# VectorE's order of work at the change to the second MLP, and the place of one ScalarE copy

## The chip, the cores and the metric

The kernel runs on one core of a Trainium2 chip. The metric is the device time of one execution in microseconds. Before the change it is 630.34 us, the median of three runs (629.96 to 630.46).

## The reference

Windowed attention with a position bias, then two layers of feed-forward work on the same 1152 tokens of 512 features. Cut to what matters:

```python
x = attention(q, k, v)                      # 1152 x 512
p = domain_probs / (domain_probs.sum(-1, keepdims=True) + 1e-09)
out = 0                                     # first MLP: 4 experts, 512 -> 1024 -> 512
for e in range(4):
    out += p[:, e:e+1] * (np.maximum(x @ w1[e], 0.0) @ w2[e])
h = out @ w_in                              # second MLP: 512 -> 2048 -> 512
g = h * np.cos(h)
return g @ w_out
```

## The kernel before, in words

Both MLPs run over groups `g` of 512 hidden features: groups 0 to 7 are the four experts (`NG1` = 8), groups 8 to 11 the second MLP. Each float32 operand is held as two parts, a rounded first part (`hi`) and the rest (`lo`); a product is three matmuls of parts (`PASSES`, L730). ScalarE makes first parts with a copy; VectorE or GpSimd makes second parts with a subtraction (`sub`, L190).

The tokens are nine tiles of 128. Tile 0 goes alone (`left`, x0). The other eight make two columns `c` = 1, 2 of 512 tokens, and the product with `w1` or `w_in` is made by seven products of 2 x 2 blocks in place of eight (`pair`). Its right-hand operands are B11, B21, B22 and the differences T1 to T4; each has two slices `m` = 0, 1 of 128 features. They lie in `xs` (B11, T2, T1, T3, B21) and `xz` (B22, T4).

**The stage of the change** is group 7 (`turn` in `steps`). There the output of the last expert is made feature by feature: `features(g, c, d)` runs 12 matmuls into one PSUM bank, for column `c` and feature block `d`; its bank is called D*cd* here, so D20 is column 2, block 0. After the matmuls VectorE multiplies by the expert's share (L1042) and adds the sum of the former experts (L1043). What follows depends on the bank, with `m = d % 2`:
- column 1 (`own`): first part of B11 (d < 2) or B21 (d >= 2), a copy of the bank to SBUF (`keep`, L1052), later the second part;
- column 2, d < 2 (`upper`): `keep`, t1 = column 2 minus column 1, T1's first and second part;
- column 2, d >= 2 (`lower`): t2, t3 on VectorE, first and second parts of T2, B22, T3, then t4 = kept value minus t2, and T4's parts.

The order is written out by hand, `(0, "D10", "f", "D20", "D12", "D22", "D11", "D21", "D13", "D23")`; "f" transposes tile 0 and makes x0. `last_flip` follows with the first products of group 8: `early[0]` (first product of pair 0), `early[1]` (of pair 1), the first half of `left`, then the second product of pair 0, the second half of `left`, the second product of pair 1. The second product adds onto the first one's bank, so it waits for ScalarE's copy `p1` of that bank (L838 in `pair`; the trace calls the tile `p`). Second products read B21; later ones T2, T1, T3, B22, T4 in that order.

Every engine runs its own instructions in the order in which the program issues them. `run` drives the steps: the step's matmuls, then `move(2)`, then `advance()` (the chains of the cosine), weight jobs, and the rest of the step. `features` issues the first piece of its generator at once and puts the generator into `moved`; `move(2)` issues up to two more pieces at the start of the next step:

```python
next(step)
move(2)
for _ in range(stages):
    advance()
for _ in range(njobs):
    next(jobs)
...
next(step, None)
```

Instructions of different engines on one PSUM bank run one after the other, in the order of issue.

Of the kernel before, what the change touches and what calls it, by code (L numbers as in the profile page):

```python
# [52 lines left out]
def tile_kernel(ctx, tc, qT, kT, v, probs, w_1, w_2, w_in, w_out, out):  # L53
    nc = tc.nc
# [134 lines left out]
    def sub(eng, out, a, b):  # L189
        eng.tensor_tensor(out=out, in0=a, in1=b, op=ALU.subtract)  # L190
# [157 lines left out]
    B11, T2, T1, T3, B21, B22, T4 = range(7)  # L348
# [62 lines left out]
    def stage(which=None):  # L411

        for st in list(staged) if which is None else [staged[which]]:
            if next(st, True):
                staged.remove(st)

    moved = []

    def move(n):

        while moved and n:
            if next(moved[0], True):
                moved.pop(0)
            else:
                n -= 1

    def split(out, src, eng):

# [275 lines left out]
    def flush():  # L704

        for out, src, hi in second_parts:
            nc.vector.scalar_tensor_tensor(  # L707
                out=out, in0=src, scalar=0.0, in1=hi.bitcast(F32), op0=ALU.max, op1=ALU.subtract
            )
        second_parts.clear()  # L710
# [38 lines left out]
    def sums():  # L749
        return bank([128, 512], "o_ps")  # L750
# [162 lines left out]
    def ahead(g, t):  # L913

        opened[g, t] = sums()
        tile_matmuls(opened[g, t], g, t, range(NFG // 2))
        yield
# [88 lines left out]
    def x_of(c, d):  # L1006

        x = accpair[:, (c - 1) * NP : c * NP].rearrange("p b (t d e) -> p (b t) d e", t=4, e=32)
        return x[:, :, d]
# [12 lines left out]
            share_rows.append(r)  # L1022

    differences = {}

    def features(g, c, d):

        flush()
        ps = sums()
        for f in range(NFG):  # L1030
            for a, bb in PASSES:
                nc.tensor.matmul(
                    ps, w_t[2, g, f // 2][:, a, f % 2, d * 128 : (d + 1) * 128],
                    hpair[:, bb, f, (c - 1) * NB : c * NB],
                    start=(f == 0 and (a, bb) == PASSES[0]),
                    stop=(f == NFG - 1 and (a, bb) == PASSES[-1]),
                )
        yield
        m, low = d % 2, d >= 2
        squares = lambda t: t.rearrange("p (t e) -> p t e", e=32)  # L1040
        x, kept = squares(ps), x_of(c, d)
        nc.vector.tensor_tensor(out=ps, in0=ps, in1=share_rows[c - 1], op=ALU.mult)  # L1042
        nc.vector.tensor_tensor(out=x, in0=x, in1=kept, op=ALU.add)  # L1043

        def hi(k, src):
            nc.scalar.activation(out=squares(operand_of_x(0, k)[:, m]), in_=src, func=AF.Copy)  # L1046

        def lo(k, src, eng):
            sub(eng, squares(operand_of_x(1, k)[:, m]), src, squares(operand_of_x(0, k)[:, m]).bitcast(F32))

        def keep():
            nc.scalar.activation(out=kept, in_=x, func=AF.Copy)  # L1052

        def difference(name):
            return squares(csp.tile([128, NB], F32, name=name, tag="c"))

        def own(k):
            hi(k, x)
            keep()
            yield  # L1060
            lo(k, x, nc.vector)

        def upper():
            keep()
            t1 = differences[m] = difference("t1")
            sub(nc.vector, t1, x, x_of(1, d))
            hi(T1, t1)
            yield
            lo(T1, t1, nc.gpsimd)

        def lower():
            t2, t3, t4 = difference("t2"), x_of(2, m), x_of(1, d)
            sub(nc.vector, t2, x, differences[m])
            sub(nc.vector, t3, x, t3)
            hi(T2, t2)
            hi(B22, x)
            yield
            lo(T2, t2, nc.gpsimd)
            lo(B22, x, nc.vector)
            hi(T3, t3)  # L1080
            yield
            lo(T3, t3, nc.gpsimd)
            sub(nc.vector, t4, t4, t2)
            hi(T4, t4)
            yield
            lo(T4, t4, nc.vector)

        ch = own(B21 if low else B11) if c == 1 else lower() if low else upper()
        next(ch)
        moved.append(ch)  # L1090

    mm = None
    count = [0]
# [23 lines left out]
    def steps(g):  # L1117

        last, turn = g == NG1 + NG2 - 1, g == NG1 - 1
        moe = g < NG1
        early_kind = 1 if g in (0, NG1) else 0 if moe else 2
        ps = [early.pop(j, None) or pair(g, j, early_kind) for j in range(2)]
        if g == 0:
            yield ahead(0, 0), 0, 0, 0
            for p in ps:
                next(p)
            seq = [0, 1, 0, 1, 0, 0, 1, 0, "0", 1, 1]
            more = [1, 1, 0, 0, 0, 0, 0, 2, 1, 0, 0]  # L1130
        elif g == NG1:
            seq = [0, 0, 0, 0, "X", 0, 1, 1, 1, "0", 1, 1]
            more = [0, 1, 1, 0, 0, 0, 0, 0, 0, 0, 0, 0]
        elif moe:
            seq = [0] * 4 + ["X"] + [0] * 3 + [1] * 7
            more = [0, 1, 1, 0, 0, 0, 0, 0] + [0, 1, 1, 1, 1, 1, 1]
        else:
            seq = [0] * 7 + ["0"] + [1] * 7
            more = [0, 1, 1, 0, 0, 0, 0, 0] + ([0] * 7 if last else [0, 1, 1, 0, 0, 0, 0])
        for j, m in zip(seq, more):  # L1140
            if j == "X":
                yield turn_rows(g), 0 if shuffled(g) else 2, m, 0
            elif j == "0":
                yield layer2(g, 0), 2, m, 0
            else:
                yield ps[j], 1, m, 0
        nxt = None if last else left(g + 1)
        ncv = {0: 2, 5: 3, 6: 3, 1: 3, "La": 3, 7: 3, 2: 3, 8: 3}
        if turn:
            order = (0, "D10", "f", "D20", "D12", "D22", "D11", "D21", "D13", "D23")  # L1150
            njobs = [2, 2, 0, 2, 2]
        elif moe:
            order = (0, 5, 6, 1, "La", "Lb", 7, 2, 8, 3, 4)
            njobs = [1] * 8
            if g == 0:
                order = (5, 6, 1, "La", "Lb", 7, 2, 8, 3, 4)
                njobs[:3] = [2, 2, 2]
                ncv = {5: 1, 6: 2, 1: 3, "La": 1, 7: 3, 2: 3, 8: 3}
        elif last:
            order, njobs = ("a5", "a6", "a7", "a8", "a1", 5, 6, 7, 8, 1, 2, 3, 4), []  # L1160
        else:
            order = ("a5", "a6", "a7", "a8", "a1", "a2", 5, 6, 7, "La", 8, "Lb", 1, 2, 3, "X", 4)
            njobs = [0, 0, 0, 0, 0, 0, 1, 1, 1, 1, 1, 1, 1, 1, 1, 1, 2]
            if g == NG1:
                njobs[4:6] = [1, 1]
        for k, o in enumerate(order):
            m = njobs.pop(0) if njobs else 0
            if nxt and shuffled(g + 1):
                if o == 2:
                    store_rows(g + 1)  # L1170
                if order[k - 1] == 2:
                    load_rows(g + 1)
            if isinstance(o, int):
                assert o == 0 or not any(c > 0 for c, _ in chains)
                yield layer2(g, o), 2, m, ncv.get(o, 0)
            elif o[0] == "f":
                yield flip(), 0, m, 0
            elif o[0] == "D":
                yield features(g, int(o[1]), int(o[2])), 2, m, 0
            elif o[0] == "a":  # L1180
                yield ahead(g, int(o[1])), 2 if last else 1, m, 0
            elif o[0] == "L":
                yield half(nxt, o == "Lb"), 2, m, ncv.get(o, 0)
            else:
                yield turn_rows(g + 1), 2, m, 0
        if turn:
            yield from last_flip(g + 1, nxt)

    def last_flip(g, nxt):

        early.update({j: pair(g, j, 1) for j in range(2)})
        yield early[0], 0, 0, 0
        yield early[1], 0, 0, 0
        yield half(nxt, False), 0, 0, 0
        yield early[0], 1, 0, 0
        yield half(nxt, True), 0, 0, 0
        yield early[1], 2, 0, 0

    def run(groups):
        for g in groups:  # L1200
            for step, stages, njobs, ncv in steps(g):
                next(step)
                move(2)
                for _ in range(stages):
                    advance()
                for _ in range(njobs):
                    next(jobs)
                for _ in range(ncv):
                    next(cv, None)
                next(step, None)  # L1210
                if g in (NG1 - 2, NG1 - 1):
                    fetch_acc(2 if g == NG1 - 2 else 0)
    with tc.manual_schedule():
# [11 lines left out]
        early = {}  # L1225
# [3 lines left out]
        def opening(j, kind):  # L1229
            early[j] = pair(0, j, kind)  # L1230
            return early[j]
# [93 lines left out]
        rest = sum(1 for _ in cv)  # L1325
# [61 lines left out]
```

## Time and profile before

| | us |
|---|---|
| median of three runs | 630.34 |
| the profiled execution | 628.96 |
| its span | 627.2 |
| TensorE busy | 615.1 |
| VectorE busy | 455.6 |
| GpSimd busy | 349.8 |
| ScalarE busy | 322.0 |

The span goes from the first to the last instruction in the profile. In the rows PE is TensorE's matmuls, PEld its weight loads, DVE VectorE, ACT ScalarE, POOL GpSimd. A timeline row gives the start, the time taken, the engine, line, operation, output<-inputs, shape and count; behind it in brackets stands how long the engine was idle before, and who ended that. Several instructions alike stand in one row.

### The profile page before, as it was taken

Reading aid. Unit: us, or ns where it says so; the run is one execution under the profiler, and the core shown is the slowest. Engines: PE = TensorE matmul, PEld = TensorE weight load, DVE = VectorE, ACT = ScalarE, POOL = GpSimd, SP = SyncE. Lnnn points to the kernel's source line nnn. Section 1 sums busy time; section 2 is a strip of 40 time slices with the busy share of each in tenths; the row PEclk is TensorE's granted clock in tenths of the full one; section 3 lists DMA queues with packets and bytes.
Section 4 is the critical chain, followed back from the end, with each engine's and each line's share of the span. In section 5 each row is a group of like instructions: output and inputs, shape, how many; then the busy total and the mean of one; then the engine's idle time right before and its main releaser. Section 6 shows DMA issues by size and latency. Waiting matters only on the chain.

```text
span 627.2 us, 9374 instructions
## 1 busy us (share of the span) xinstructions
PE 615.1 (98%) x3348; PEld 504.1 (80%) x3348; DVE 455.6 (73%) x783; ACT 322.0 (51%) x674; POOL 349.8 (56%) x332
## 2 busy tenths in 40 slices
PE   8999999999999999999999999996999999999998
PEld 6777888888888888888888888884878888888886
DVE  6878898689799799698698645667574664664663
ACT  6989444434434444434442521544783683673660
POOL 4868495463573464464554561673359479379340
PEclk9999999999999999999999999998999999999999
DMA  9641236256348158157163237420101202202003
GB/s 269 176 157 40 93 120 190 56 155 221 94 153 268 49 173 264 38 179 205 36 215 120 66 102 222 147 68 1 34 1 35 100 0 68 67 1 68 15 4 134
DMA packets 51246, 69.05 MB, mean 110 GB/s; under 512 B 6912, under 2 KB 31488, under 8 KB 51200
## 3 DMA queue, kind: packets, MB, share of 16 engines
q1 hardware_dynamic: 50656, 68.06, 35.0%
q8 instruction: 26, 0.43, 0.3%
q10 hardware_dynamic: 544, 0.39, 0.2%
q14 instruction: 20, 0.16, 0.1%
HBM read 53.76 MB, written 14.68 MB: 109 GB/s over the span
## 4 chain that ended last, share of the span: by engine, by line
PE 90%; DVE 4%; ACT 4%; POOL 1%; issue 1%; ACTq 0%; DVEq 0%; POOLq 0%
PE o_ps L923 43%; PE o_ps L730 35%; PE o_ps L784 5%; PE x_ps L571 2%; PE t_ps L535 1%; PE s_ps L465 1%; DVE o_ps L1043 1%; DVE o_ps L1042 1%; PE r_ps L509 1%; PE o_ps L1219 1%; ACT p L484 1%; ACT xs L1046 1%; ACT accpair L1052 1%; DVE xs L190 0%; PE o_ps L963 0%
## 5 line engine op out<-in xcount | busy, mean ns | idle before, releaser
L923 PE MATMUL o_ps<-w2t,hpair 128*128 128x512 f32 x1044 | 241.4, 389 | 0.0
L923 PEld LDWEIGHTS o_ps<-w2t,hpair 128*128 128x128 f32 x1044 | 195.7, 188 | 40.6
L730 PE MATMUL o_ps<-xs,w1t 128*128 128x512 f32 x720 | 170.2, 392 | 6.0 <-ACT p L838 6.0
L730 PEld LDWEIGHTS o_ps<-xs,w1t 128*128 128x128 f32 x720 | 135.5, 189 | 35.2 <-ACT p L838 6.4
L190 POOL TENSOR_TENSOR w2t<-raw,w2t 128x512 fp32r<-128x512 f32 x48 | 63.5, 1338 | 78.5 <-ACT w2t L214 78.4
L190 POOL TENSOR_TENSOR w1t<-raw,w1t 128x512 fp32r<-128x512 f32 x48 | 64.5, 1362 | 62.0 <-ACT w1t L214 61.6
L190 POOL TENSOR_TENSOR w1t<-sm,w1t 128x512 fp32r<-128x512 f32 x48 | 63.8, 1346 | 31.3 <-ACT w1t L214 31.0
L730 PE MATMUL o_ps<-xz,w1t 128*128 128x512 f32 x288 | 69.8, 390 | 0.1
L190 POOL TENSOR_TENSOR hpair<-u,hpair 128x512 fp32r<-128x512 f32 x30 | 40.2, 1348 | 52.4 <-ACT hpair L688 52.4
L313 ACT ACTIVATE cr<-cr 128x512 f32<-128x512 f32 x32 | 21.7, 679 | 81.7 <-DVE ca L307 81.7
L730 PEld LDWEIGHTS o_ps<-xz,w1t 128*128 128x128 f32 x288 | 53.8, 188 | 11.8 <-DVE c L832 0.7
L707 DVE SCALAR_TENSOR_TENSOR hpair<-o_ps,hpair 128x512 fp32r<-128x512 f32 x47 | 32.3, 688 | 19.2 <-ACT hpair L716 19.1
L716 ACT ACTIVATE hpair<-o_ps 128x512 fp32r<-128x512 f32 x47 | 28.0, 595 | 33.6 <-DVE o_ps L832 33.5
L214 ACT ACTIVATE w1t<-sm 128x512 fp32r<-128x512 f32 x44 | 27.6, 629 | 32.6 <-POOL sm L190 32.6
L944 DVE SCALAR_TENSOR_TENSOR accpair<-o_ps,pr,accpair 128x512 f32<-128x512 f32 x48 | 34.8, 745 | 10.4 <-PE o_ps L923 10.4
L672 DVE SCALAR_TENSOR_TENSOR u<-r,u 128x512 f32<-128x512 f32 x36 | 28.1, 781 | 15.9 <-ACT r L669 15.9
L784 PE MATMUL o_ps<-w1t,x 128*128 128x512 f32 x144 | 36.0, 393 | 0.0
L952 DVE TENSOR_TENSOR accpair<-o_ps,accpair 128x512 f32<-128x512 f32 x23 | 15.7, 689 | 27.8 <-PE o_ps L923 27.8
L832 DVE TENSOR_TENSOR o_ps<-o_ps,u 128x512 f32<-128x512 f32 x48 | 33.1, 692 | 3.0 <-PE o_ps L730 2.8
L923 PE MATMUL o_ps<-w2t,h 128*128 128x512 f32 x144 | 34.7, 389 | 0.0
L316 DVE SCALAR_TENSOR_TENSOR co<-cr,ca 128x512 f32<-128x512 f32 x32 | 33.4, 1043 | 1.4 <-ACT cr L313 0.4
L484 ACT ACTIVATE p<-p,nmax 128x192 f32<-128x192 f32 (+1 forms) x72 | 31.0, 436 | 4.7 <-DVE nmax L478 4.6
(147 smaller groups left out, 892.8 us busy)
## 6 DMA issues: line engine op xcount, KB each, us to landing
raw<-w SPq DMA_DIRECT2D x32, 512.0 KB, 4.4
cr<-w_in SPq DMA_DIRECT2D x16, 512.0 KB, 4.5
cr<-w_out SPq DMA_DIRECT2D x16, 512.0 KB, 4.2
wi<-co SPq DMA_DIRECT2D x16, 256.0 KB, 3.4
wo<-co SPq DMA_DIRECT2D x16, 256.0 KB, 2.2
raw<-wi SPq DMA_DIRECT2D x8, 512.0 KB, 3.5
raw<-wo SPq DMA_DIRECT2D x8, 512.0 KB, 3.7
qt<-qT SPq DMA_DIRECT2D x8, 256.0 KB, 4.2
```

Source lines behind the costliest of these rows:

```text
L190: eng.tensor_tensor(out=out, in0=a, in1=b, op=ALU.subtract)
L214: nc.scalar.activation(out=out, in_=src, func=AF.Copy)
L316: nc.vector.scalar_tensor_tensor(out=fl(o), in0=fl(hw), scalar=TINY, in1=fl(a), op0=ALU.is_ge, op1=ALU.mult,)
L484: nc.scalar.activation(out=p[:, k], in_=p[:, k], func=AF.Exp, scale=-1.0, bias=nmax[:, k : k + 1], accum_out=den[:, k, 0:1],)
L672: nc.vector.scalar_tensor_tensor(out=u, in0=r, scalar=MAGIC, in1=u, op0=ALU.subtract, op1=ALU.subtract)
L707: nc.vector.scalar_tensor_tensor(out=out, in0=src, scalar=0.0, in1=hi.bitcast(F32), op0=ALU.max, op1=ALU.subtract)
L716: nc.scalar.activation(out=hi, in_=src, func=AF.Relu)
L730: nc.tensor.matmul(ps, w(a, k, m), operand_of_x(bb, b)[:, m], start=(start and m == 0 and (a, bb) == PASSES[0]), stop=(stop and m == 1 and ...
L784: nc.tensor.matmul(ps.rearrange("p (j f) -> p j f", j=2), x0[:, bb, d, :], w1[:, :, a, 0, d * 256 : (d + 1) * 256], start=(d == 0 and (a, ...
L832: add = lambda out, a, b: nc.vector.tensor_tensor(out=out, in0=a, in1=b, op=ALU.add)
L923: nc.tensor.matmul(ps, hidden(a, f, t), w_t[2, g, f // 2][:, bb, f % 2, :], start=(f == 0 and (a, bb) == PASSES[0]), stop=(f == NFG - 1 an ...
L944: nc.vector.scalar_tensor_tensor(out=o, in0=ps, scalar=s, in1=o, op0=ALU.mult, op1=ALU.add)
```

## The change

`moved` and `move` go, so no pieces are issued ahead of a bank's own work. A bank's sums and differences are issued first; second parts are put into a list, `seconds`, and `second_of_before()` issues the former bank's at a fixed place behind the sums. In `upper`'s case `keep` now comes after the difference. B21's second part of slice 1 is made by GpSimd, from the kept copy; T4's second parts are made by GpSimd too. The last bank, D23, stops after its differences (`yield`), and `opening` in `last_flip` issues the copy of pair 0's first product first, then the rest of D23.

```diff
--- before.py
+++ after.py
@@ -413,16 +413,6 @@
         for st in list(staged) if which is None else [staged[which]]:
             if next(st, True):
                 staged.remove(st)
-
-    moved = []
-
-    def move(n):
-
-        while moved and n:
-            if next(moved[0], True):
-                moved.pop(0)
-            else:
-                n -= 1
 
     def split(out, src, eng):
 
@@ -1022,6 +1012,11 @@
             share_rows.append(r)
 
     differences = {}
+    seconds = []
+
+    def second_of_before():
+        while seconds:
+            seconds.pop(0)()
 
     def features(g, c, d):
 
@@ -1054,40 +1049,42 @@
         def difference(name):
             return squares(csp.tile([128, NB], F32, name=name, tag="c"))
 
-        def own(k):
+        if c == 1:
+            second_of_before()
+            k = B21 if low else B11
             hi(k, x)
             keep()
-            yield
-            lo(k, x, nc.vector)
-
-        def upper():
-            keep()
+            if low and m:
+                lo(k, kept, nc.gpsimd)
+            else:
+                seconds.append(lambda: lo(k, x, nc.vector))
+        elif not low:
             t1 = differences[m] = difference("t1")
             sub(nc.vector, t1, x, x_of(1, d))
+            second_of_before()
             hi(T1, t1)
-            yield
+            keep()
             lo(T1, t1, nc.gpsimd)
-
-        def lower():
+        else:
             t2, t3, t4 = difference("t2"), x_of(2, m), x_of(1, d)
             sub(nc.vector, t2, x, differences[m])
             sub(nc.vector, t3, x, t3)
+            second_of_before()
+            if m:
+                yield
             hi(T2, t2)
             hi(B22, x)
-            yield
+            hi(T3, t3)
             lo(T2, t2, nc.gpsimd)
-            lo(B22, x, nc.vector)
-            hi(T3, t3)
-            yield
             lo(T3, t3, nc.gpsimd)
-            sub(nc.vector, t4, t4, t2)
-            hi(T4, t4)
-            yield
-            lo(T4, t4, nc.vector)
-
-        ch = own(B21 if low else B11) if c == 1 else lower() if low else upper()
-        next(ch)
-        moved.append(ch)
+
+            def rest():
+                lo(B22, x, nc.vector)
+                sub(nc.vector, t4, t4, t2)
+                hi(T4, t4)
+                lo(T4, t4, nc.gpsimd)
+
+            seconds.append(rest)
 
     mm = None
     count = [0]
@@ -1176,7 +1173,8 @@
             elif o[0] == "f":
                 yield flip(), 0, m, 0
             elif o[0] == "D":
-                yield features(g, int(o[1]), int(o[2])), 2, m, 0
+                last_features = features(g, int(o[1]), int(o[2]))
+                yield last_features, 2, m, 0
             elif o[0] == "a":
                 yield ahead(g, int(o[1])), 2 if last else 1, m, 0
             elif o[0] == "L":
@@ -1184,12 +1182,20 @@
             else:
                 yield turn_rows(g + 1), 2, m, 0
         if turn:
-            yield from last_flip(g + 1, nxt)
-
-    def last_flip(g, nxt):
+            yield from last_flip(g + 1, nxt, last_features)
+
+    def last_flip(g, nxt, last_features):
 
         early.update({j: pair(g, j, 1) for j in range(2)})
-        yield early[0], 0, 0, 0
+
+        def opening():
+            next(early[0])
+            yield
+            next(early[0])
+            next(last_features, None)
+            second_of_before()
+
+        yield opening(), 0, 0, 0
         yield early[1], 0, 0, 0
         yield half(nxt, False), 0, 0, 0
         yield early[0], 1, 0, 0
@@ -1200,7 +1206,6 @@
         for g in groups:
             for step, stages, njobs, ncv in steps(g):
                 next(step)
-                move(2)
                 for _ in range(stages):
                     advance()
                 for _ in range(njobs):
```

## Rows read from the trace of the kernel before

**Rows 1.** The page, busy time of the engines: us, share of the span, instructions.

```profile
PE 615.1 (98%) x3348; PEld 504.1 (80%) x3348; DVE 455.6 (73%) x783; ACT 322.0 (51%) x674; POOL 349.8 (56%) x332
```

**Rows 2.** Waits of TensorE: engine, line, releaser, us in total, times, longest.

```profile
PE o_ps L730 <- ACT p L838: 6.0, 1, 6.0
```

**Rows 3.** TensorE's timeline around the change to group 8.

```profile
409.49 19.32 PE L1032 MATMUL o_ps<-hpair,w2t 128*128 128x512 f32 x84
428.64 2.88 PE L730 MATMUL o_ps<-xs,w1t 128*128 128x512 f32 x12
431.37 1.52 PE L784 MATMUL o_ps<-w1t,x 128*128 128x512 f32 x6
438.87 2.93 PE L730 MATMUL o_ps<-xs,w1t 128*128 128x512 f32 x6 [5.98 <-ACT p L838]
441.59 1.81 PE L784 MATMUL o_ps<-w1t,x 128*128 128x512 f32 x6
443.24 5.62 PE L730 MATMUL o_ps<-xs,w1t 128*128 128x512 f32 x24
448.70 1.53 PE L730 MATMUL o_ps<-xz,w1t 128*128 128x512 f32 x6
```

**Rows 4.** Busy time and granted clock (PEclk) by stretch; x counts instructions.

```profile
core 0: us, PE busy (x) PEld busy (x) DVE busy (x) ACT busy (x) POOL busy (x), PEclk, DMA share, GB/s
409.30:428.80 19.50, 19.50 (x89) 16.19 (x88) 14.50 (x22) 9.58 (x18) 11.96 (x11) 1.00 0.19 55
...
434.00:435.00 1.00, 0.00 (x0) 0.00 (x0) 0.97 (x2) 0.00 (x0) 0.00 (x0) 1.00 0.00 0
435.00:436.00 1.00, 0.00 (x0) 0.00 (x0) 0.70 (x2) 0.86 (x2) 0.15 (x1) 0.65 0.00 0
...
441.00:442.00 1.00, 1.00 (x3) 0.73 (x3) 0.00 (x0) 0.17 (x1) 0.00 (x0) 0.50 0.00 0
```

**Rows 5.** VectorE's timeline: the start of the stage, and bank D23.

```profile
411.92 0.69 DVE L190 TENSOR_TENSOR xs<-o_ps,xs 128x512 fp32r<-128x512 f32 x1 [1.15 <-ACT accpair L1052]
...
415.21 0.69 DVE L190 TENSOR_TENSOR t<-o_ps,accpair 128x512 f32<-128x512 f32 x1 [0.67 <-ACT accpair L1052]
...
432.95 0.69 DVE L1042 TENSOR_TENSOR o_ps<-o_ps,share 128x512 f32<-128x512 f32 x1
433.68 0.70 DVE L1043 TENSOR_TENSOR o_ps<-o_ps,accpair 128x512 f32<-128x512 f32 x1
434.41 0.69 DVE L190 TENSOR_TENSOR t<-o_ps,t 128x512 f32<-128x512 f32 x1
435.02 0.68 DVE L190 TENSOR_TENSOR accpair<-o_ps,accpair 128x512 f32<-128x512 f32 x1
436.37 0.69 DVE L190 TENSOR_TENSOR xz<-o_ps,xz 128x512 fp32r<-128x512 f32 x1 [0.66 <-ACT xz L1046]
436.97 0.69 DVE L190 TENSOR_TENSOR accpair<-accpair,t 128x512 f32<-128x512 f32 x1
438.36 0.98 DVE L190 TENSOR_TENSOR xz<-accpair,xz 128x512 fp32r<-128x512 f32 x1 [0.69 <-ACT xz L1046]
```

**Rows 6.** ScalarE's timeline behind bank D23.

```profile
435.14 0.63 ACT L1046 ACTIVATE xs<-t 128x512 fp32r<-128x512 f32 x1 [2.82 <-DVE t L190]
435.74 0.60 ACT L1046 ACTIVATE xz<-o_ps 128x512 fp32r<-128x512 f32 x1
...
437.70 0.63 ACT L1046 ACTIVATE xz<-accpair 128x512 fp32r<-128x512 f32 x1 [0.84 <-DVE accpair L190]
438.23 1.07 ACT L838 ACTIVATE p<-o_ps 128x512 f32<-128x512 f32 x2
```

**Rows 7.** GpSimd's timeline: T1's second part, and T3's.

```profile
430.59 1.29 POOL L190 TENSOR_TENSOR xs<-t,xs 128x512 fp32r<-128x512 f32 x1 [5.47 <-ACT xs L1046]
...
437.08 1.71 POOL L190 TENSOR_TENSOR xs<-accpair,xs 128x512 fp32r<-128x512 f32 x1
```

**Rows 8.** TensorE's weight loads, the next wait after the stage.

```profile
458.99 2.61 PEld L730 LDWEIGHTS o_ps<-xz,w1t 128*128 128x128 f32 x12 [0.56 <-DVE c L832]
```

## The prediction

> **What bounds the kernel now.** I read the busy times first, then TensorE's waits, then the stretch around the one long wait on all engines. TensorE is busy 98% of the span [rows 1], so only its own idle time or its speed can be worth anything. Its waits hold one of 6.0 us, for ScalarE's copy `p` in `pair` (L838) [rows 2]. It lies exactly where the diff works.
>
> On TensorE's timeline [rows 3] the 84 matmuls of the last seven banks of `features` run without a gap from 409.49 to 428.64, which is 0.228 us each or 2.74 us a bank. The last bank, D23, ends at 409.49 + 19.32 = 428.81; the banks before it end 2.74 us apart: D13 at 426.07, D21 at 423.33, D11 at 420.59, D22 at 417.85, D12 at 415.11, D20 at 412.38. Then come the first products of both pairs (12 matmuls) and the first half of `left` (6), and the next matmul could start at 431.37 + 6 × 0.228 = 432.74. It starts at 438.87: **6.13 us lost**. The wait has a second price. The granted clock is 1.00 before it, 0.65 on the mean of 435 to 436, and still 0.50 (the 1.2 GHz level of the two) in 441 to 442 [rows 4]. The 12 matmuls from 438.87 to 443.24 take 4.37 us; at 0.228 us each they would take 2.74: **1.63 us lost**. From 443.24 the next 24 need 448.70 − 443.24 = 5.46 us, full speed again.
>
> Why the copy is late: it stands on ScalarE's queue behind all that D23 issues [rows 6], and D23's chain starts late on VectorE. D23's matmuls end at 428.81, but its first instruction (L1042) runs at 432.95 [rows 5], 4.1 us later. VectorE isn't short of time, it is busy for 14.50 of 19.50 us while that backlog grows [rows 4]. It stands in front of small waits on ScalarE: 1.15 us for the second part of B11 behind `keep`, 0.67 us for t1 behind `keep` [rows 5], and seven more like these follow, the last two of 0.66 and 0.69 us. The first of them waits for `keep`, which reads the same PSUM bank, and not only for its own first part.
>
> **The change, part by part.** *Order on VectorE.* In `run` the two pieces that `move(2)` issued ahead of a bank's own sums go. Now a bank's product, sum and differences come first, and the former bank's second parts after them; by then their first parts are long done. I count the new order with two steps from rows: 0.73 us to a dependent instruction (432.95, 433.68, 434.41) and 0.61 us to an independent one (434.41, 435.02) [rows 5].
> - From 412.4: x0's second part 0.61, D20's two sums 0.73 + 0.73, t1 0.61, second part of B11 0.61, D12's sums 0.73 + 0.70: free at 417.1, before D12's successor D22 ends at 417.85.
> - D22 from 417.9: 0.73 + 0.73 + 0.61 + 0.61 and B21's second part 0.61: 421.2.
> - D11 from 421.2: 0.73 + 0.61, then D22's rest (B22's second part, t4) 0.61 + 0.61: 423.8.
> - D21's sums end at 425.2. t1 needs D11's `keep`, which stands on ScalarE behind the first parts of T4 and B11: t4 ends at 423.8, then 0.53 + 0.50 + 0.60 gives 425.5. So t1 waits 0.3 us, B11's second part starts at 426.1, D13's sums end at 428.1.
>
> So VectorE is free 0.7 us before D23's matmuls end, and D23's L1042 runs at 428.85 (0.04 after its matmuls), **4.1 us earlier** than now. No second part comes too late: the first product at 428.64 wants B11's second part, which ends at 426.8, with 1.8 us to spare.
>
> *Work that changes engine.* The second part of the lower B21 (m = 1) and both of T4 go from VectorE (0.69 us) to GpSimd (1.29 us alone, 1.71 us beside VectorE [rows 7]). B21's: D13's sums end 428.1, first part and `keep` end 429.2, GpSimd ends between 430.6 and 431.0. It is wanted at 432.74 by the second product of pair 0: covered with at least 1.7 us. T4's is third in GpSimd's queue after T2 and T3, from 431.7, so it ends at 435.6 to 436.8, and no product reads T4 before the five that follow 435.5 + 1.37: covered. T2 is wanted first of those, from 436.8, and is done by 433.5.
>
> *The copies.* `opening` issues pair 0's copy ahead of D23's first parts. The product ends at 428.64 + 6 × 0.228 + 0.17 = 430.18 (0.17 is what the 84 matmuls take beyond 84 × 0.228), ScalarE is free since 429.2, so the copy ends at 430.8; the second product at 432.74 no longer waits for it. Pair 1's copy is now the one behind D23. D23's chain keeps its steps: from L1042 to the copy's start it was 438.23 − 432.95 = 5.28 us [rows 5, 6], where T4's first part is the last link. From 428.85 this gives 434.13, and TensorE went on 0.64 us after that start: 434.77. Pair 1's second product can start at 432.74 + 2.74 = 435.48. The spare time is 0.7 us, the thinnest of all.
>
> *DMAs, jobs, SP.* None is issued, moved or passed; the weight jobs keep their place. SP's queue is untouched.
>
> *After the turn.* ScalarE is free at 434.7, when pair 0's second product has ended at 434.3: its first chain starts up to 0.5 us late, on work that TensorE reads much later. The nearest later wait is 0.56 us of the weight load for `c22` at 458.99 [rows 8]; it stays, as TensorE and its feeders move together. It could grow by those 0.5 us or vanish (0.28 us of matmul time).
>
> **Sum.** 6.13 + 1.63 = 7.76; I take 7.7 off. The profiled execution took 628.96 us (span 627.2 and 1.76 around it), which makes 621.3. It lies 1.38 below the median of 630.34; against the median the forecast is 622.6. Bounds: gain 8.3 (the wait at 458.99 goes, small steps shorter) to 5.7 (rivals 1 and 2).
>
> One price is doubtful, VectorE beside GpSimd. Now t4 took its usual 0.69 us at 436.97 although GpSimd's next piece ran beside it from 437.08 on, but T4's second part on VectorE took 0.98 instead of 0.69 beside GpSimd's 1.71 [rows 5, 7]. From this I take t4 at 0.69 and 0.3 us for a clash.
> The Trainium skill, page SBUF — State Buffer, section "Who interferes with whom", says that a VectorE instruction with two SBUF inputs and a GpSimd instruction that reads SBUF exclude each other, the later one blocked until the first ends. It speaks against moving parts to GpSimd. The stretched 0.98 and 1.71 agree with it, the unstretched t4 does not.
>
> **Rivals.**
> 1. *The wait moves to pair 1's copy.* t4 would be held for a whole GpSimd piece, T3's: 1.29 us on the chain to 434.77 gives 436.06, against 435.48: 0.58 us of wait, no fall of the clock (now it fell some 2.5 us into the wait). Time 623.2. (The Trainium skill, SBUF — State Buffer, "Who interferes with whom", would have it so whenever T3's piece starts first.) Another microsecond of backlog on VectorE would add one: 624.2. For it: the spare 0.7 us is the end of a long chain. Against: t4 now runs unstretched. 15%.
> 2. *The copy gains nothing by its place* (pair 0's copy still ends the wait, for example if the order on ScalarE's queue came out as before). Then only the 4.1 us of VectorE count: TensorE waits 2.0 us, too short for the clock to fall, time 630.34 − 4.1 − 1.63 = 624.6. 5%.
> 3. *The change does not do what it says on VectorE:* banks still start as late, only the copy is early. Then pair 0 waits 0.35 us for B21's part and pair 1's copy still ends at 438.8, against 435.8: 3.35 us of wait, gain 2.8 to 4.4, time 625.9 to 627.5. Against it: the diff issues the sums first, and VectorE runs in the order of issue. 2%.
> 4. *Slower: the deferred second part of B11.* It now comes after t1, which waits for D11's `keep`, which waits behind T4's first part, which waits for t4: three engines in a ring of hand-offs, ahead of the first product. Its spare time is 1.8 us. It decides from there on; to lose it has to slip by 1.8 + 7.7 = 9.5 us, then 630.34 and more, for instance 632 at a slip of 11. The waits of that kind that the rows show are 0.66 to 1.15 us each, so eight at once. 1%, and 1% for the like in a buffer's release.
>
> **How the numbers follow.** Forecast as worked out 74%, rivals 15, 5, 2 and 2, the last 2% no change at all. The range goes from 630.34 − 8.3 = 622.0, less 0.4 for the spread of the runs, 621.6, to rival 2 with the same kind of margin, 624.8. A measurement can tell about 0.2% (1.3 us) of this kernel from no change; the forecast and the first three rivals are all beyond it. Faster 0.96, same 0.02, slower 0.02.
>
> **What would show it.** TensorE's wait for L838 gone or below 0.6 us; 36 matmuls after the first half of `left` at 0.228 us each and a granted clock of 1.00 from 409 on; D23's first sum within 0.1 us of the end of its matmuls, no wait of VectorE for `keep` but one of 0.3 us before t1; the first copy at about 430.2, the second at about 434.1, T4's first part the instruction before it. A wait of TensorE for L838 at about 435.5 would be rival 1; one at 432.74 of 2 us rival 2; a first sum of D23 after 430 would show the count on VectorE wrong; a wait ahead of the first product rival 4. A gain that is there at 450 and gone at the end would show a bound behind this stage that I have not seen.

## The result and the profile after

The changed kernel takes 622.08 us (median of 4 runs, 620.9 to 622.35) against 630.15 in the runs of before beside it: a ratio of 0.9871, 95% interval 0.9854 to 0.9888. The forecast was 622.6, the range 621.6 to 624.8.

The page of the profile after, busy times; TensorE has 99% of the span in place of 98% [rows 1]:

```profile
PE 613.9 (99%) x3348; PEld 503.4 (81%) x3348; DVE 453.0 (73%) x780; ACT 321.5 (52%) x674; POOL 353.0 (57%) x335
```

The waits of TensorE after, the longest two; the 6.0 us for the copy [rows 2] are gone from the list, and what leads it now lies at the start of the kernel:

```profile
PE o_ps L1224 <- DVE dens L1222: 1.2, 1, 1.2
PE r_ps L499 <- POOL wide L491: 0.5, 2, 0.3
```

TensorE's timeline after, the same stretch as [rows 3]; L720 is the L730 of before, L774 its L784:

```profile
410.06 19.34 PE L1027 MATMUL o_ps<-hpair,w2t 128*128 128x512 f32 x84
429.23 2.88 PE L720 MATMUL o_ps<-xs,w1t 128*128 128x512 f32 x12
431.95 1.52 PE L774 MATMUL o_ps<-w1t,x 128*128 128x512 f32 x6
433.31 1.52 PE L720 MATMUL o_ps<-xs,w1t 128*128 128x512 f32 x6
434.67 1.52 PE L774 MATMUL o_ps<-w1t,x 128*128 128x512 f32 x6
436.03 5.60 PE L720 MATMUL o_ps<-xs,w1t 128*128 128x512 f32 x24
441.47 1.52 PE L720 MATMUL o_ps<-xz,w1t 128*128 128x512 f32 x6
```

Every group starts where the one before it leaves off: from 429.23 to 441.47 there are 12.24 us for 54 matmuls, 0.227 us each, the rate of the 84 before them (0.228). To compare kernels I use one length, the **stage**: from the first of the 84 matmuls to the first matmul on `hpair` in group 8. TensorE's timelines before and after have that end at:

```profile
461.87 12.40 PE L923 MATMUL o_ps<-w2t,hpair 128*128 128x512 f32 x54
```

```profile
454.60 12.40 PE L913 MATMUL o_ps<-w2t,hpair 128*128 128x512 f32 x54
```

Before, the stage is 461.87 − 409.49 = 52.38 us, after 454.60 − 410.06 = 44.54 us: **7.84 us less**, against a sum of 7.76. The two profiled spans differ by 7.2, since the stage starts 0.57 us later in the profile after; up to there both kernels issue the same work, and the start of the stage lies between 409.13 and 410.33 in all kernels of this study.

Busy time and granted clock after, in the stretch of the old wait and the one behind it (columns as in [rows 4], the clock is the third from the right):

```profile
432.80:438.90 6.10, 6.10 (x28) 5.05 (x28) 2.71 (x4) 5.06 (x11) 3.79 (x3) 1.00 0.00 0
438.90:445.00 6.10, 6.10 (x31) 5.05 (x30) 5.66 (x9) 4.70 (x10) 2.76 (x3) 1.00 0.12 33
```

VectorE's timeline after; 429.43 to 433.46 is bank D23, the counterpart of 432.95 to 436.97 in [rows 5]:

```profile
415.04 0.69 DVE L190 TENSOR_TENSOR t<-o_ps,accpair 128x512 f32<-128x512 f32 x1
...
426.24 0.69 DVE L190 TENSOR_TENSOR t<-o_ps,accpair 128x512 f32<-128x512 f32 x1 [0.33 <-ACT accpair L1047]
...
429.43 0.70 DVE L1037 TENSOR_TENSOR o_ps<-o_ps,share 128x512 f32<-128x512 f32 x1 [0.57 <-PE o_ps L1027]
430.17 0.70 DVE L1038 TENSOR_TENSOR o_ps<-o_ps,accpair 128x512 f32<-128x512 f32 x1
430.90 0.69 DVE L190 TENSOR_TENSOR t<-o_ps,t 128x512 f32<-128x512 f32 x1
431.51 0.68 DVE L190 TENSOR_TENSOR accpair<-o_ps,accpair 128x512 f32<-128x512 f32 x1
432.85 0.69 DVE L190 TENSOR_TENSOR xz<-o_ps,xz 128x512 fp32r<-128x512 f32 x1 [0.67 <-ACT xz L1041]
433.46 0.72 DVE L190 TENSOR_TENSOR accpair<-accpair,t 128x512 f32<-128x512 f32 x1
```

D23's matmuls end at 410.06 + 19.34 = 429.40, and its first sum runs 0.03 us later. VectorE waited 0.57 us for it: now VectorE waits for TensorE there, not the other way. ScalarE and GpSimd after, the counterparts of [rows 6, 7]:

```profile
431.13 0.60 ACT L828 ACTIVATE p<-o_ps 128x512 f32<-128x512 f32 x1 [1.14 <-PE o_ps L720]
431.62 0.63 ACT L1041 ACTIVATE xs<-t 128x512 fp32r<-128x512 f32 x1
...
434.21 0.63 ACT L1041 ACTIVATE xz<-accpair 128x512 fp32r<-128x512 f32 x1 [0.88 <-DVE accpair L190]
434.75 0.58 ACT L828 ACTIVATE p<-o_ps 128x512 f32<-128x512 f32 x1
...
430.07 1.30 POOL L190 TENSOR_TENSOR xs<-accpair,xs 128x512 fp32r<-128x512 f32 x1 [1.10 <-ACT accpair L1047]
...
433.59 1.74 POOL L190 TENSOR_TENSOR xs<-accpair,xs 128x512 fp32r<-128x512 f32 x1
```

The two copies stand apart now, one ahead of D23's first parts and one behind them. TensorE's second product of pair 1 starts at 436.03; before, it went on 0.64 us after the start of the copy, so the second copy (434.75) leaves 0.64 us to spare.

### The profile page after: what moved, and what is told of

Same layout as the page of the kernel before. It is cut to its first block, busy times and chain, and to the rows that moved or that the text cites. A ratio compares the mean times of both kernels' runs of the same rounds, so it can differ in the third digit from the quotient of the medians.

```text
span 620.0 us, 9378 instructions
## 1 busy us (share of the span) xinstructions
PE 613.9 (99%) x3348; PEld 503.4 (81%) x3348; DVE 453.0 (73%) x780; ACT 321.5 (52%) x674; POOL 353.0 (57%) x335
## 4 chain that ended last, share of the span: by engine, by line
PE 94%; ACT 2%; DVE 2%; POOL 1%; issue 1%; ACTq 0%; POOLq 0%; DVEq 0%
PE o_ps L913 43%; PE o_ps L720 35%; PE o_ps L774 5%; PE o_ps L1027 4%; PE x_ps L561 2%; PE t_ps L525 1%; PE s_ps L455 1%; PE r_ps L499 1%; PE o_ps L1224 1%; PE o_ps L953 0%; ACT u L658 0%; ACT r L659 0%; POOL w1t L190 0%; DVE p L468 0%; ACT u L666 0%
## 5 line engine op out<-in xcount | busy, mean ns | idle before, releaser
L720 PE MATMUL o_ps<-xs,w1t 128*128 128x512 f32 x720 | 168.8, 390 | 0.0
L720 PEld LDWEIGHTS o_ps<-xs,w1t 128*128 128x128 f32 x720 | 134.8, 188 | 28.6 <-issue 0.5
L720 PE MATMUL o_ps<-xz,w1t 128*128 128x512 f32 x288 | 69.8, 390 | 0.1
L720 PEld LDWEIGHTS o_ps<-xz,w1t 128*128 128x128 f32 x288 | 53.8, 188 | 11.8 <-DVE c L822 0.7
L774 PE MATMUL o_ps<-w1t,x 128*128 128x512 f32 x144 | 35.7, 391 | 0.0
```

The lines of the kernel that those rows point to most:

```text
L720: nc.tensor.matmul(ps, w(a, k, m), operand_of_x(bb, b)[:, m], start=(start and m == 0 and (a, bb) == PASSES[0]), stop=(stop and m == 1 and ...
L774: nc.tensor.matmul(ps.rearrange("p (j f) -> p j f", j=2), x0[:, bb, d, :], w1[:, :, a, 0, d * 256 : (d + 1) * 256], start=(d == 0 and (a, ...
```

## The experiments

Theory: the wait had two causes in a row, VectorE's backlog (4.1 us) and the copy's place on ScalarE's queue, and each part of the change removes one; behind the wait stands a second cost, the clock. Rivals: one part does it all; the parts moved to GpSimd or the place of `keep` matter; pair 1's copy has no room. Times are medians; the stage is from the profile of each kernel. The kernel before took 629.80 us beside e1 to e4 and 629.22 beside e5 and the d runs, so each ratio is to the before of its own runs, and kernels are compared with each other by the stage.

| kernel | us | stage | over the changed kernel's stage |
|---|---|---|---|
| before | 630.15 | 52.38 | 7.84 |
| changed | 622.08 | 44.54 | |
| e1, copy alone | 626.38 | 49.70 | 5.16 |
| e2, order alone | 624.99 | 48.38, again 48.36 | 3.84, 3.82 |
| e3, parts on VectorE | 621.31 | 44.56 | 0.02 |
| e4, keep first | 622.23 | 44.53 | −0.01 |
| e5, part ahead of t4 | 622.47 | 45.33 | 0.79 |
| d2, 2 copies more | 622.54 | 45.36 | 0.82 |
| d4, 4 copies more | 624.19 | 46.68, again 48.33 | 2.14, 3.79 |
| d8, 8 copies more | 629.45 | 50.80, again 52.58 and 52.62 | 6.26, 8.04, 8.08 |

**e1, the copy's place alone,** on the kernel before. `lower` stops after its differences in D23, and the copy is issued ahead of the pieces:

```diff
+            if m:
+                yield
             hi(T2, t2)
...
-        yield early[0], 0, 0, 0
+        def opening():
+            next(early[0])
+            next(early[0])
+            yield
+        yield opening(), 0, 0, 0
```

> The kernel before with one part of the change: pair 0's copy goes ahead of D23's first parts; banks keep the old order on VectorE. My theory (both parts are needed, each worth what the chain after it leaves): D23's first sum stays about 4.1 us behind its matmuls; TensorE waits about 0.35 us for B21's second part ahead of pair 0's second product, then about 3.0 us for pair 1's copy, which still stands behind T4's first part; the clock falls about 2.5 us into that wait. Time 626 to 627.5. Rival, the copy's place is all: no wait over 0.6 us, 622.5. Rival, the order on VectorE is all: 630.

Measured: 626.38 us, ratio 0.9946 (0.9931 to 0.996). VectorE's and TensorE's timelines of e1, and its busy time and clock where the clock fell:

```profile
433.20 0.69 DVE L1042 TENSOR_TENSOR o_ps<-o_ps,share 128x512 f32<-128x512 f32 x1
...
433.10 1.66 PE L730 MATMUL o_ps<-xs,w1t 128*128 128x512 f32 x6
...
439.11 7.36 PE L730 MATMUL o_ps<-xs,w1t 128*128 128x512 f32 x24 [2.96 <-ACT p L838]
```

```profile
439.00:439.50 0.50, 0.40 (x1) 0.36 (x2) 0.50 (x1) 0.50 (x2) 0.03 (x1) 0.79 0.00 0
```

D23's first sum is 4.1 us behind its matmuls (409.75 + 19.34 = 429.09), as before. Pair 0's second product no longer waits for its copy; it loses about 0.2 us (0.09 at its start, 0.14 inside) to B21's second part. Pair 1's second product waits instead, and 24 matmuls after it take 7.19 us to the next group's start (446.30) where 5.47 would do: the clock, 1.7 us. So the copy's place alone moves the wait one product on. The theory's time holds, and its waits within 0.15 us (0.2 for 0.35, 3.1 for 3.0); both rivals fall. Its clock does not: it was to fall about 2.5 us into the wait, but was still 1.00 up to 439.0 and fell at about 439.3, when TensorE was back (439.11).

**e2, the order alone,** on the changed kernel:

```diff
             yield
-            next(early[0])
             next(last_features, None)
             second_of_before()
+            next(early[0])
```

> The changed kernel with the other part alone: VectorE's new order, but both copies behind D23's parts as before. My theory: D23's first sum follows its matmuls at once; TensorE waits about 2.0 us for pair 0's copy, too short for the clock to fall; 622.1 + 2.0 = 624.1, the remaining wait of pair 1's copy hidden. Rival, the copy's place is all: 630. Rival, the order on VectorE is all: 622.1.

Measured: 624.99 us, ratio 0.9921 (0.9902 to 0.994), so 0.9 more than expected, with runs from 623.12 to 626.13. TensorE's timeline of e2, and its busy time and clock by stretch:

```profile
434.52 2.87 PE L720 MATMUL o_ps<-xs,w1t 128*128 128x512 f32 x6 [1.91 <-ACT p L828]
437.19 1.95 PE L774 MATMUL o_ps<-w1t,x 128*128 128x512 f32 x6
```

```profile
432.50:434.50 2.00, 0.12 (x1) 0.00 (x0) 0.82 (x2) 1.15 (x3) 2.00 (x3) 1.00 0.00 0
434.50:435.00 0.50, 0.48 (x1) 0.44 (x2) 0.00 (x0) 0.46 (x1) 0.50 (x1) 0.62 0.00 0
435.00:438.00 3.00, 3.00 (x8) 2.31 (x7) 0.00 (x0) 0.58 (x1) 0.68 (x1) 0.50 0.00 0
```

The wait is the 2.0 us of the theory (431.09 + 1.37 = 432.46 to 434.52). But the clock is 1.00 throughout the wait and falls **after** TensorE has started again; the 12 matmuls from 434.52 take 438.98 − 434.52 = 4.46 us instead of 2.74. "Too short for the clock to fall" was wrong. I profiled it a second time.

> The order on VectorE alone, a second time, to see the clock. In its first profile TensorE's wait of 2.0 us was followed by a fall of the granted clock just after TensorE had started again, and its runs spread from 623.1 to 626.1. My theory now: the wait itself is fixed (1.9 us), whether the clock falls after it differs from run to run: either about 2.74 us for the next 12 matmuls and a stage of 46.6 us from the first of the 84 matmuls to the first of `ahead`, or about 4.4 us and 48.4. Rival: the fall belongs to this kernel and comes each time, 48.4.

Measured: wait 1.91, stage 48.36, 12 matmuls in 4.45 us: it fell again. Both profiles would fit the rival (each time), but the other runs on record don't: the granted clock, as a mean over the span, is 0.997 in three of e2's four timed runs (624.97 to 626.13 us; one of them is the first profile) and 1.000 in the fourth, 623.12 us, 1.9 us under the median. That one went without the fall, so the rival falls and the theory, from run to run, holds.

**e3, the second parts back on VectorE,** on the changed kernel:

```diff
-            if low and m:
-                lo(k, kept, nc.gpsimd)
-            else:
-                seconds.append(lambda: lo(k, x, nc.vector))
+            seconds.append(lambda: lo(k, x, nc.vector))
...
-                lo(T4, t4, nc.gpsimd)
+                lo(T4, t4, nc.vector)
```

> The changed kernel with the second parts of B21 (slice 1) and of T4 made by VectorE again, in the new order. My theory: they lie in VectorE's spare time (B21's behind D23's differences, done about 0.5 us before it is wanted; T4's long before), so 622.1 within 0.6 us and no wait of TensorE. Rival, VectorE's work itself ends the stage: two of the three parts on the chain, 2 x 0.69, so 623.5.

Measured: 621.31 us, ratio 0.9866 (0.9851 to 0.9881); the stage is that of the changed kernel within 0.02 us, and the lower median isn't the stage's. Moving the parts to GpSimd buys no time. It buys room. VectorE's (D23's first sum), ScalarE's and TensorE's timelines of e3:

```profile
429.00 0.69 DVE L1037 TENSOR_TENSOR o_ps<-o_ps,share 128x512 f32<-128x512 f32 x1
...
434.31 0.58 ACT L828 ACTIVATE p<-o_ps 128x512 f32<-128x512 f32 x1
...
435.11 5.61 PE L720 MATMUL o_ps<-xs,w1t 128*128 128x512 f32 x24
```

The second copy starts 0.80 us ahead of the product that needs it, in the changed kernel 1.28: the spare time falls from 0.64 to 0.16 us, because D23's first sum now runs 0.53 us behind its matmuls (409.13 + 19.34 = 428.47). So the parts do not lie wholly in VectorE's spare time, as expected: what did not fit was taken in by the spare time of the copy.

**e4, `keep` ahead of the difference t1 again,** on the changed kernel:

```diff
+            keep()
             t1 = differences[m] = difference("t1")
...
-            keep()
```

> The changed kernel with `keep` ahead of the difference t1 again, as before the change. My theory: t1 waits some 0.5 to 0.7 us more in each slice, but VectorE waits 0.88 us for D22's matmuls and 0.57 us for D23's, which take that in: 622.1 within 0.6 us, D23's first sum within 0.2 us of where it was. Rival, every such wait was on the path: 2 x 0.67 more, 623.4.

Measured: 622.23 us, ratio 0.9876 (0.986 to 0.9893). VectorE's timeline of e4, D21's t1 and D23's first sum:

```profile
426.69 0.69 DVE L190 TENSOR_TENSOR t<-o_ps,accpair 128x512 f32<-128x512 f32 x1 [0.82 <-ACT accpair L1047]
...
429.41 0.70 DVE L1037 TENSOR_TENSOR o_ps<-o_ps,share 128x512 f32<-128x512 f32 x1
```

t1 waits 0.82 us instead of 0.33, and D23's first sum still runs 0.04 us after its matmuls (410.05 + 19.32 = 429.37): the wait for D23 took it in. The place of `keep` brings nothing here; the rival falls. No run takes back the place of `keep` and the parts on GpSimd together: each uses up spare time that the other also needs (0.49 us of VectorE's 0.57 here, 0.48 of the copy's 0.64 in e3), so together they may cost time.

**d2, d4 and d8, more work ahead of the second copy,** on the changed kernel, with 2, 4 or 8 in place of n. The copies repeat T4's first part:

```diff
                 hi(T4, t4)
+                for _ in range(n * m):
+                    hi(T4, t4)
```

> The changed kernel with T4's first part of slice 1 made three times (2 more ScalarE copies of 0.6 us ahead of pair 1's copy). My theory: pair 1's copy has 0.64 us to spare, beyond that TensorE waits one for one: 1.2 - 0.64 = 0.6 us of wait, 622.7. Rival, ScalarE has ample room there: no wait, 622.1. Rival, any wait costs the clock too: 0.6 + 1.6, 624.3.

> The same with 4 more copies, 2.4 us. My theory: 1.76 us of wait, the granted clock stays 1.00, 623.9. Rival, any wait costs the clock: 625.5.

> The same with 8 more copies, 4.8 us. My theory: 4.2 us of wait, the clock falls about 2.5 us into it and comes back some 3 us of matmuls later, which costs up to 1.6 us more: 622.1 + 5.8 = 627.9; without the clock's part it would be 626.3.

Measured: d2 622.54 us (ratio 0.9896, 0.9879 to 0.9912), d4 624.19 (0.9929, 0.9912 to 0.9946), d8 629.45 (1.0001, 0.9992 to 1.0011). TensorE's timeline of d2, of d4, and of d4 a second time, each the product that waits for the second copy:

```profile
436.31 5.74 PE L720 MATMUL o_ps<-xs,w1t 128*128 128x512 f32 x24 [0.52 <-ACT p L828]
```

```profile
438.08 5.74 PE L720 MATMUL o_ps<-xs,w1t 128*128 128x512 f32 x24 [1.85 <-ACT p L828]
```

```profile
437.46 7.36 PE L720 MATMUL o_ps<-xs,w1t 128*128 128x512 f32 x24 [1.85 <-ACT p L828]
```

The second copy's delay is what ScalarE's timeline of d8 shows, nine copies in a row, (5.92 − 0.63) / 8 = 0.66 us apart and not the 0.6 I had taken:

```profile
434.47 5.92 ACT L1041 ACTIVATE xz<-accpair 128x512 fp32r<-128x512 f32 x9 [0.88 <-DVE accpair L190]
```

Less the 0.64 us to spare, 2, 4 and 8 copies should then hold TensorE for 0.68, 2.00 and 4.64 us. It starts 0.67 us after the end of the group before it in d2 (434.27 + 1.37 to 436.31), 2.00 in d4 and 4.64 in d8: beyond the spare time it waits one for one. d2's stage is 0.82 us longer, d4's 2.14; the 0.14 beyond the wait lies in the 24 matmuls behind it (5.57 and 5.58 us to the next group, in the changed kernel 5.44). The second profile of d4 is for the clock.

> Four extra copies, a second time. In its first profile a wait of the same 2.0 us was followed by no fall. My theory now: the wait is 1.85 us again; the clock stays, with a stage of 46.7 us, or falls, with 48.3. Rival: it never falls in this kernel, 46.7.

With the same wait of 1.85 us the clock stayed at 1.00 the first time, and the second time the same 24 matmuls took 7.36 us in place of 5.74: stage 48.33, both numbers of the expectation. Same kernel, same wait, 1.65 us apart. So the clock's part of a wait of this length is not fixed by the kernel, and the rival "never" falls. The mean clock of d4's four timed runs agrees: 0.999 and above in three (623.96 to 624.35 us), 0.997 in the one at 625.90. What decides it from run to run was not tried.

d8 took more than expected, 629.45 for 627.9, and its first profile (628.71 us; the next expectation says 628.3) lies under the median. Two more profiles:

> Eight extra copies, a second time; its first profile took 628.3 (stage 50.8 us, 1.6 of it the clock's) while the median of its runs is 629.45. My theory now: the wait is 4.5 us again and the rest is the clock's, which may be low for longer here than in the first profile: up to 3.3 us for the clock, stage 52.5. Rival: the stage takes 50.8 again and the difference lies outside it.

> Eight extra copies, a third time, with the same expectation as the second: wait 4.5 us, stage between 49.2 us (no fall) and 52.5 us (the clock low for longer than in the first profile); rival 50.8 each time.

TensorE's timeline of d8 in the first and the second profile:

```profile
440.93 7.23 PE L720 MATMUL o_ps<-xs,w1t 128*128 128x512 f32 x24 [4.49 <-ACT p L828]
```

```profile
440.26 8.38 PE L720 MATMUL o_ps<-xs,w1t 128*128 128x512 f32 x24 [4.48 <-ACT p L828]
```

Busy time and clock by stretch of the second profile:

```profile
439.00:440.00 1.00, 0.00 (x0) 0.00 (x0) 0.00 (x0) 0.97 (x3) 0.20 (x1) 0.54 0.00 0
440.00:445.00 5.00, 4.74 (x11) 3.78 (x12) 1.38 (x2) 4.12 (x9) 1.07 (x1) 0.50 0.00 0
445.00:446.00 1.00, 1.00 (x4) 0.73 (x4) 0.22 (x1) 1.00 (x3) 0.00 (x0) 0.55 0.00 0
```

The wait is 4.5 us in all three. In the first the clock fell near the end of the wait (the 24 matmuls take 7.07 us to the next group, 1.6 over); in the second it fell at about 439.1, before TensorE was back at 440.26, and stayed at 0.50 until about 445.9 (8.41 us, 2.9 over). The third has nearly the stage of the second, 52.62. d8's ten timed runs split the same way: four at a mean clock of 0.997 took 628.27 to 628.71 us, six at 0.994 or 0.995 took 629.40 to 629.99. Against the first expectation of d8 the wait is 0.4 us longer, by the 0.66 us a copy, and the clock costs up to 1.3 us more. The expected 49.2 to 52.5 held but for 0.1, and the rival (50.8 each time) falls.

**e5, t4 behind the start of GpSimd's piece,** on the changed kernel: B22's second part made twice.

```diff
                 lo(B22, x, nc.vector)
+                if m:
+                    lo(B22, x, nc.vector)
                 sub(nc.vector, t4, t4, t2)
```

> The changed kernel with B22's second part of slice 1 made twice, so that t4 starts about 0.6 us later and GpSimd's piece for T3 begins before it. My theory: t4 takes 0.7 to 0.8 us beside GpSimd, pair 1's copy comes 0.6 us later and just in time, TensorE waits less than 0.1 us, 622.1. Rival 1 of the prediction (a piece of GpSimd holds t4 until it ends): t4 ends at the end of T3's piece, 0.8 us later still, and TensorE waits about 0.8 us, 622.9.

Measured: 622.47 us, ratio 0.9896 (0.9881 to 0.991), stage 0.79 us longer. Timelines of VectorE (t4), GpSimd (T3's piece) and TensorE of e5:

```profile
433.69 1.25 DVE L190 TENSOR_TENSOR accpair<-accpair,t 128x512 f32<-128x512 f32 x1
...
433.10 1.29 POOL L190 TENSOR_TENSOR xs<-accpair,xs 128x512 fp32r<-128x512 f32 x1
...
436.15 5.78 PE L720 MATMUL o_ps<-xs,w1t 128*128 128x512 f32 x24 [0.44 <-ACT p L828]
```

Here my theory fell and rival 1's mechanism showed: TensorE waits 0.60 us (434.18 + 1.37 = 435.55 to 436.15), for less than 0.1 by the theory and 0.8 by the rival. When GpSimd's piece starts first (433.10), it takes its plain 1.29 us and t4 takes 1.25 in place of 0.72. In the changed kernel t4 starts first (433.46 against 433.59), t4 takes 0.72 and GpSimd's piece 1.74. The one that starts second pays about 0.5 us. t4 ends 0.55 us after GpSimd's piece, a little less than its own plain duration, so it was held to about that piece's end. T4's second part in the kernel before shows the same: it ends 0.55 us after the piece beside it (438.36 + 0.98 against 437.08 + 1.71 [rows 5, 7]). The Trainium skill, SBUF — State Buffer, section "Who interferes with whom", says that a VectorE instruction with two SBUF inputs contends with a GpSimd instruction that reads SBUF, and that the order of issue decides which of two is blocked. The 1.25 us of t4 in e5 and the 1.74 us of GpSimd's piece in the changed kernel agree with it.

## Why the prediction was right

- **VectorE's order, 4.1 us:** D23's first sum follows its matmuls by 0.03 us, before 4.14. The count of steps held within 0.2 us: t1 of D21 was to wait 0.3 us and waited 0.33, and VectorE was to be free 0.7 us before D23's matmuls end and waited 0.57 for them. e1, which keeps the old order, keeps the 4.1 us.
- **The copy's place:** the first copy starts 1.90 us after the start of the first product (429.23 to 431.13), 0.4 us later than forecast (430.18 − 428.64 = 1.54), with 1.5 us to spare (431.13 + 0.64 against 433.31); why was not followed up. The second starts 5.32 us after D23's first sum (429.43 to 434.75; forecast 5.28). Neither holds TensorE. e2, without the new place, waits the 2.0 us of rival 2.
- **The clock, 1.63 us:** 1.00 throughout, and the 12 matmuls after the old wait at the full rate.
- **Sum:** 7.76 forecast before rounding, 7.84 us in the stage. The median moved by 8.07.
- **No second bound:** the weight loads' wait for `c22`, 0.56 us before [rows 8], is 0.56 us after. The spans differ by 7.2 us and the stage starts 0.57 us later: 7.77 of the 7.84 reach the end. Weight loads of TensorE after:

```profile
451.75 2.59 PEld L720 LDWEIGHTS o_ps<-xz,w1t 128*128 128x128 f32 x12 [0.56 <-DVE c L822]
```

- **The thin spare time:** forecast 0.7 us, read as 0.64, and the waits of d2, d4 and d8 fit 0.64.

Two side steps failed, and neither moved the sum. Rival 2's price took the clock to stay up after a wait of 2.0 us ("too short for the clock to fall"): e2 showed a fall in both profiles, some 1.7 us, so its 624.6 would have been 626.3 in such a run. And the doubt about t4 was settled the wrong way: it ran unstretched before and after because it started first (by 0.11 and 0.13 us), not because the two engines don't hold each other, as e5 showed. The unstretched t4 was therefore no evidence against the engines' excluding each other, as the prediction took it. t4 is on the chain to the second copy, so that its price of 0.69 us came out right (0.72) rests on a lead of 0.13 us that the forecast had not counted: luck. Had GpSimd's piece started just ahead of t4, at 433.46, and held it as in e5, t4 would have ended at about 433.46 + 1.29 + 0.55 = 435.30, 1.1 us later than it did, and TensorE would have waited about 0.5 us; that is an estimate from these rows, and no run has it.

What was not forecast: two of the four edits, each taken back by itself, bring no time. The parts on GpSimd (e3) and the place of `keep` (e4) leave the stage where it is. The gain is VectorE's order and the copy's place together: alone, the first leaves 3.8 of the 7.84 us in the stage, the second 5.2.

## What to carry to other kernels

When one engine waits for the last instruction of a queue, count two things apart: how late that queue's chain starts, and what stands ahead of the awaited instruction on its queue; here each alone left a wait of 2 to 3 us, and in nearly every run the fall of the clock with it. Issue a bank's own sums ahead of the former bank's leftovers, so that an in-order engine meets work whose inputs are long done. Price a TensorE wait of 2 us at 2 us or at 3.7, since the clock may fall even after TensorE is back.

## What the runs showed of the hardware that was not expected

- The granted clock can fall after TensorE has resumed: in e2 it was 1.00 up to 434.5, TensorE started at 434.52, and the clock was 0.50 from about 434.6 to 438. In the other falls behind waits of 2 to 3 us it also came after TensorE was back, by 0.2 us (e1), 0.8 (e2 again) and 1.3 (d4 again). Nor does it come at one time into a longer wait: 2.6 us in the kernel before (432.74 to 435.3), 3.5 in the second profile of d8, 4.4 in the first.
- The same wait in the same kernel costs the clock or not: d4 with 1.85 us of wait took 5.74 us for 24 matmuls in one profile and 7.36 in another; d8 with 4.5 us paid 1.6 us in its 24 matmuls in one and 2.9 in another.
- A VectorE subtraction with both inputs in SBUF and a GpSimd subtraction hold each other, and the one that starts second pays: t4 0.72 or 1.25 us, GpSimd's piece 1.74 or 1.29, by which of them started 0.1 to 0.6 us ahead.
